# Chunked complex attention with a routed expert layer: expert weights loaded before the last units, factors gathered as rows, gates kept in place

## The chip, the cores and the metric

One core of one Trainium2 chip. The metric is device time of one execution in microseconds; the kernel before takes 468.15 us (median of 3 runs, 465.80 to 468.39).

## The reference

Two layers follow each other. The first is a recurrence with complex gates over 768 steps, for 4 batches x 8 heads of 48 channels; the second routes each of the 3072 tokens to at most one of 8 experts.

```python
mag = sqrt(a_re**2 + a_im**2);  scale = minimum(mag, 0.999) / (mag + 1e-6)
for t in range(768):              # S is complex, 48 x 48 for each batch and head
    S = (a_re + 1j*a_im)[t] * scale[t] * S + outer(k[t], v[t])
    y[t] = q[t] @ S.real
x = y as (3072, 384)
do = x @ w_skip > 0;  e = argmax(x @ w_gate);  g = softmax(x @ w_gate)[e]
out = x;  out[do] = x + g * (relu(x @ w1[e]) @ w2[e])   # w1: 384 x 1024, w2: 1024 x 384
```

## The kernel before, in words

**Units.** The sequence is cut into 6 chunks of 128 steps; a unit u = 4*c + b is one chunk c of one batch b, all 8 heads. Within a chunk the recurrence becomes matmuls: `pre(u)` (L158) loads the gates and turns them into log sizes U and a ratio r (Ln, Exp, a Square on ScalarE at L172, Ln, Exp; VectorE in between, with the test of L174 that marks gates too large for this path); `angle(u)` (L181) takes the arctangent of the ratio, sums it over the chunk with a matmul (L188) and makes sines and cosines cs; `size(u)` (L209) sums U with a matmul (L214) and makes e = exp(+-sum). `ready(u)` (L221) loads q and k, multiplies them by e (L232) and cs (L234) and transposes the results (tp, L239; copied by ScalarE at L240). `unit(u)` (L248) does the products: pa (L261) masked into at (L262), the state T carried over the chunks (RX L268, st L270, ps L274, T L277), py (L285, L288), and px (L293), which gives the output rows xa and the router's logits.

**Factors.** `factors(c)` (L199) needs the last row (step 127) of e and cs of the four units of a chunk, turned so that channels lie on partitions. L197 and L219 write those rows to DRAM, and six DMAs per chunk (L203, L205) read them back into G one 4-byte element at a time; L207 multiplies them into Fall, which the next chunk's RX reads.

**Order.** ScalarE's tables are switched twice per batch of four units: one phase for Ln and Exp (pre, size), one for Arctan and Sin (angle). Every piece gets a due time in units (`add(time, function)`, L475 on, with the gates AHEAD = 3 units before their own unit) and a scheduler turns due times and readiness into one instruction order per engine. SP issues all plain DMAs in one in-order queue; POOL issues the indirect ones.

**Routing and experts.** `route(c)` (L325) routes four units in one series of small VectorE operations; for the chunks that `last(c)` names (before: 4 and 5) `route1` (L389) does it unit by unit. Each ends in indirect DMAs on POOL (L322) that scatter the rows xa into the list xs, one after the other. px, ps and pr (the ranks within an expert) share one PSUM buffer (`ps_g`, tag g). In the first `route1` of chunk 5, `early` (L319) loads expert 0's first rows back from xs. `end` frees the gates' pools (ld, fe), in whose place m0 and mr come: `weights(0)` (L539) then loads expert 0's weights in seven pieces through two raw buffers (L551); ScalarE rounds each (L555), VectorE takes the remainder (L556). `tokens` (L568) collects expert 0's tokens by one-hot products (L591), and `moe` (L597) runs the experts: L620 and L643 to L645.

Of the kernel before, what the change touches and what calls it, by code (L numbers as in the profile page):

```python
# [9 lines left out]
F32 = mybir.dt.float32  # L10
# [15 lines left out]
BATCH = 4  # L26
AHEAD, TRIG, READY = 3.0, 1.0, 0.7
# [13 lines left out]
class Kern:  # L41
# [12 lines left out]
    def consts(self, ctx):  # L54
# [49 lines left out]
        self.G = cst.tile([96, NCH, 3, BH], F32, name="G")  # L104
# [53 lines left out]
    def pre(self, u):  # L158

        nc = self.nc  # L160
        V, A = nc.vector, nc.scalar
# [13 lines left out]
        V.scalar_tensor_tensor(la, la, 2.0, tr[:, 0], ALU.mult, ALU.add)  # L175
        self.table(tr[:, 0], la, AF.Exp, scale=-0.5, bias=self.lnw)
        U = self.U[u] = self.fe.tile([128, H, D], F32, name=f"U_{u}", tag="U", bufs=2 * BATCH)
        V.scalar_tensor_tensor(U, la, 0.0, tr[:, 0], ALU.min, ALU.subtract)
        self.tr[u] = tr

    def angle(self, u):  # L181
# [11 lines left out]
        cs = self.cs[u] = self.fe.tile([128, H, 2, D], F32, name=f"cs_{u}", tag="cs", bufs=BATCH + 2)  # L193
# [3 lines left out]
        nc.sync.dma_start(self.turns_at[c, b:b + 1], cs[127:128].rearrange("o h k d -> o (h k d)"))  # L197

    def factors(self, c):  # L199

        for r in range(2):
            g = self.G[r * D:(r + 1) * D, c]
            self.nc.sync.dma_start(g[:, 0], self.sizes_at[c].rearrange("b (h d) -> d (b h)", d=D))  # L203
            for k in range(2):
                self.nc.sync.dma_start(g[:, 1 + k], self.turns_at[c].rearrange("b (h k d) -> k d (b h)", d=D, k=2)[k])  # L205
        e = self.G[:, c, 0].unsqueeze(1).to_broadcast([96, 2, BH])
        self.nc.vector.tensor_tensor(self.Fall[:, c].rearrange("p k b h -> p k (b h)"), self.G[:, c, 1:3], e, ALU.mult)  # L207

    def size(self, u):  # L209

        nc = self.nc
        U = self.U.pop(u)
        pl = self.ps_c.tile([128, H, D], F32, name=f"pl_{u}", tag="c")
        nc.tensor.matmul(pl, self.mask, U, start=True, stop=True)  # L214
        e = self.e[u] = self.fe.tile([128, 2, H, D], F32, name=f"e_{u}", tag="e", bufs=BATCH)
# [3 lines left out]
        nc.sync.dma_start(self.sizes_at[c, b:b + 1], e[127:128, 0].rearrange("o h d -> o (h d)"))  # L219

    def ready(self, u):  # L221
# [4 lines left out]
        qk = self.ld.tile([128, 2, H, D], F32, name=f"qk_{u}", tag="qk", bufs=3)  # L226
# [17 lines left out]
    def last(self, c):  # L244

        return c // 2 == NG - 1

    def unit(self, u):  # L248
# [16 lines left out]
        if c > 0:  # L265
# [4 lines left out]
            V.scalar_tensor_tensor(Sb[:, :, 0:D], X[:, 1], self.sg, X[:, 0], ALU.mult, ALU.add)  # L270
# [184 lines left out]
    def attention(self):  # L455
        with ExitStack() as ctx:
# [4 lines left out]
            self.un, self.st = P("un", 2), P("st", 2)  # L461
# [7 lines left out]
            self.pr_ins, self.T, self.U, self.tr, self.cs, self.e, self.w = [{} for _ in range(7)]  # L469
# [27 lines left out]
            for k, us in enumerate(batches + [[]]):  # L497
# [16 lines left out]
            for k in range(1, 9):  # L514
                add(k // 3 + 0.2 + 0.25 * (k % 3), self.late, k)
            flat = [b[0] - AHEAD + 0.4 for b in batches]
            for u in range(n):
                if u not in batches[-1]:
                    add(u - READY, self.ready, u)
                else:  # L520
                    for k in range(2):
                        add(u + 0.5 + 0.25 * k, lambda: next(self.ws, None))
# [133 lines left out]
    def check(self, p, ps):  # L656
# [5 lines left out]
        with self.tc.issue_after(self.pins[1]):  # L662
# [10 lines left out]
            V.tensor_scalar(ok[:, 0, 0:B * NCH], self.over, 0.0, None, ALU.is_equal)  # L673
# [191 lines left out]
```

## Time and profile before

| | |
|---|---|
| median of 3 runs | 468.15 us |
| profiled execution, its own time | 470.65 us |
| its span, first to last instruction | 468.9 us |
| busy: PE / weight loads / VectorE / ScalarE / POOL | 396.7 / 351.4 / 330.3 / 299.7 / 66.4 us |
| DMA | 207010 packets, 68.77 MB; 184779 packets under 512 B |
| mean granted TensorE clock | 0.945 of full speed |

PE is TensorE's matmuls, PEld its weight loads (they overlap the matmuls), DVE VectorE, ACT ScalarE, SP the queue that issues DMAs. A matmul's shown length includes its way through the array, so that rows overlap; what one costs in a dense stretch is the distance from start to start. A bracket at a row's end is the idle time of its engine ahead of it, and what ended it. Line numbers L... are those of the kernel before; in the changed one the same code stands up to 5 lines lower or higher.

### The profile page before, as it was taken

The numbers are of one execution on the slowest core, as the hardware profiler recorded it, in microseconds if no ns is written. First come the engines' busy times: TensorE is split into PE (matmuls) and PEld (weight loads), VectorE is DVE, ScalarE is ACT, GpSimd is POOL, SyncE is SP. The second block draws the span as 40 slices with busy tenths as digits, with TensorE's granted clock in tenths as the row PEclk, the third lists the DMA queues.
The fourth block names the chain that finished last, engine by engine and source line by source line (L and its number), as shares of the span: only waits on it lengthen the run. The fifth ranks groups of instructions, "written<-read, shape, count | busy, mean of one in ns | idle before, by whom it ended". The sixth has DMA issues, their size and how long they took to land. (4 is left out here: it accounts for less than half of the span.)

```text
span 468.9 us, 8930 instructions
## 1 busy us (share of the span) xinstructions
PE 396.7 (85%) x3179; PEld 351.4 (75%) x3179; DVE 330.3 (70%) x780; ACT 299.7 (64%) x591; POOL 66.4 (14%) x94
## 2 busy tenths in 40 slices
PE   0698946999898989988997974498869999999994
PEld 0387832898787779767966863498869999999993
DVE  3467567987997898879979883447883667667331
ACT  6889859798978887896897262126652446446220
POOL 6000000000412012001201222200411010111011
PEclk9969967999999999999999996599989999999998
DMA  9999894992899489758507462356882685685000
GB/s 141 223 274 186 118 169 45 140 188 71 123 169 176 50 126 190 153 49 152 119 20 66 131 204 80 104 202 182 281 264 86 214 286 161 209 287 152 21 25 29
DMA packets 207010, 68.77 MB, mean 147 GB/s; under 512 B 184779, under 2 KB 202855, under 8 KB 206960
## 3 DMA queue, kind: packets, MB, share of 16 engines
q1 hardware_dynamic: 204400, 63.51, 62.9%
q0 software_dynamic: 2560, 4.63, 2.8%
q8 instruction: 27, 0.44, 0.4%
q14 instruction: 23, 0.19, 0.1%
HBM read 52.55 MB, written 15.88 MB: 146 GB/s over the span
## 5 line engine op out<-in xcount | busy, mean ns | idle before, releaser
L555 ACT CAST h<-r 128x768 fp32r<-128x768 f32 (+1 forms) x56 | 49.7, 925 | 37.1 <-DMA r<-in_moe_w_dram 20.9
L556 DVE TENSOR_TENSOR l<-r,h 128x768 fp32r<-128x768 f32 (+1 forms) x56 | 58.2, 1070 | 21.2 <-ACT h L555 21.0
L322 POOL DMA_INDIRECT xs<-xa,sl x24 | 32.0, 1333 | 232.1 <-ACT e L156 85.9
L239 PE MATMUL tp<-ident,w 128*96 128x128 f32 x384 | 56.7, 286 | 9.4 <-ACT wT L240 4.0
L240 ACT COPY wT<-tp 96x512 f32<-96x512 f32 x96 | 53.6, 591 | 14.6 <-PE tp L239 10.2
L239 PEld LDWEIGHTS tp<-ident,w 128*96 128x96 f32 x384 | 43.7, 132 | 19.5 <-ACT wT L240 8.5
L620 PE MATMUL ph<-xh,h 128*128 128x256 f32 x192 | 54.0, 287 | 4.3 <-DVE hl L623 3.7
L622 ACT ACTIVATE hh<-ph 128x256 fp32r<-128x256 f32 x64 | 23.5, 382 | 50.9 <-PE ph L620 48.0
L261 PE MATMUL pa<-wT,wT 96*128 96x128 f32 x384 | 53.4, 286 | 1.6 <-ACT wT L240 1.6
L620 PE MATMUL ph<-xh,l 128*128 128x256 f32 x192 | 53.8, 285 | 0.0
L261 PEld LDWEIGHTS pa<-wT,wT 96*128 96x128 f32 x384 | 47.9, 197 | 6.2 <-ACT wT L240 2.8
L620 PE MATMUL ph<-xl,h 128*128 128x256 f32 x192 | 51.5, 284 | 0.0
L285 PE MATMUL py<-at,vt 128*64 128x128 f32 x384 | 39.3, 292 | 9.1 <-DVE at L262 6.2
L234 DVE TENSOR_TENSOR w<-qk,cs 128x768 f32<-128x768 f32 x48 | 44.9, 947 | 0.0
L643 PE MATMUL po<-h,hh 128*128 128x384 f32 x128 | 44.0, 344 | 0.0
L644 PE MATMUL po<-l,hh 128*128 128x384 f32 x128 | 43.4, 339 | 0.0
L623 DVE SCALAR_TENSOR_TENSOR hl<-ph,hh 128x256 fp32r<-128x256 f32 x64 | 25.5, 418 | 25.4 <-ACT hh L622 24.4
L620 PEld LDWEIGHTS ph<-xh,h 128*128 128x128 f32 x192 | 36.6, 191 | 5.3 <-DVE hl L623 4.5
L293 PE MATMUL px<-wg,yT 128*128 128x105 f32 x192 | 28.2, 293 | 13.8 <-DVE m L420 10.8
L645 PE MATMUL po<-h,hl 128*128 128x384 f32 x128 | 39.7, 338 | 0.0
L293 PEld LDWEIGHTS px<-wg,yT 128*128 128x128 f32 x192 | 25.7, 206 | 16.0 <-DVE m L420 11.1
L620 PEld LDWEIGHTS ph<-xh,l 128*128 128x128 f32 x192 | 36.8, 191 | 0.0
(157 smaller groups left out, 831.3 us busy)
## 6 DMA issues: line engine op xcount, KB each, us to landing
r<-in_moe_w_dram SPq DMA_DIRECT2D x24, 512.0 KB
r<-in_moe_w_dram SPq DMA_DIRECT2D x32, 384.0 KB
ain<-in_a_re_dram SPq DMA_DIRECT2D x24, 192.0 KB
ain<-in_a_im_dram SPq DMA_DIRECT2D x24, 192.0 KB
qk<-in_q_dram SPq DMA_DIRECT2D x24, 192.0 KB
qk<-in_k_dram SPq DMA_DIRECT2D x24, 192.0 KB
vt<-in_v_dram SPq DMA_DIRECT2D x24, 192.0 KB
out_dram<-xa SPq DMA_DIRECT2D x24, 192.0 KB
```

The source lines that it names most:

```text
L234: V.tensor_tensor(n, qk[:, k].unsqueeze(2).to_broadcast([128, H, 2, D]), cs, ALU.mult)
L239: nc.tensor.transpose(tp[:, h], n[:, hh * 4 + h].rearrange("p k d -> p (k d)"), self.ident)
L240: A.copy(t[:, hh * 4:hh * 4 + 4], tp)
L261: PE.matmul(pa[:, h], kT[:, hh * 4 + h], qT[:, hh * 4 + h], start=True, stop=True)
L285: PE.matmul(py[j * 64:j * 64 + 64, hp], vt_[:, 2 * hp + j], at[:, 2 * hp + j], start=True, stop=(c == 0))
L293: pe = PE.matmul(px[:, hp], yT[:, hp], self.wg[:, hp], start=True, stop=True)
L555: nc.scalar.copy(hi[:, ks], raw)
L556: nc.vector.tensor_tensor(lo[:, ks], raw, hi[:, ks], ALU.subtract)
L620: pe = PE.matmul(ph, w[:, k, js], x[:, k], start=(n == 0), stop=(n == len(terms) - 1))
L643: PE.matmul(po, hh[:, j, sl], w2h[:, j], start=(j == 0), stop=False)
L644: PE.matmul(po, hh[:, j, sl], w2l[:, j], start=False, stop=False)
L645: pe = PE.matmul(po, hl[:, j, sl], w2h[:, j], start=False, stop=(j == NF - 1))
```

## The change

The gates' intermediate results go in place (into ain and tr) instead of la and sq; the square and the test become one VectorE instruction with a running maximum, and `check` compares that maximum at the end. q and k are multiplied by e in one instruction. The last rows go straight into an SBUF tile G of 4 partitions (each twice), and 24 transposes of 4 x 96 per chunk turn them; two ScalarE copies, one with the sign sg, and one VectorE product make Fall, so that st is a plain sum. AHEAD is 4. qk, cs and e move to a pool ff that outlives the gates; `end` and `weights(0)` come due from 16.5 units on, and only chunk 5 is routed unit by unit.

```diff
-AHEAD, TRIG, READY = 3.0, 1.0, 0.7
+AHEAD, TRIG, READY = 4.0, 1.0, 0.7
...                                     # pre: ain 6 buffers (4)
-        self.table(la, ain[:, 0], AF.Ln)
-        self.table(sq[:, 1], la, AF.Exp, scale=-1.0)
-        V.tensor_tensor(tr[:, 1], ain[:, 1], sq[:, 1], ALU.mult)
-        A.activation(sq[:, 0], tr[:, 1], AF.Square)
-        self.table(tr[:, 0], sq[:, 0], AF.Ln, scale=WIDE, bias=self.wide)
-        V.tensor_scalar(sq[:, 1], sq[:, 0], 2.4, None, ALU.is_gt, ALU.add, accum_out=self.over[:, u:u + 1])
+        re, im, s, r = ain[:, 0], ain[:, 1], tr[:, 0], tr[:, 1]
+        self.table(re, re, AF.Ln)
+        self.table(s, re, AF.Exp, scale=-1.0)
+        V.tensor_tensor(r, im, s, ALU.mult)
+        V.tensor_tensor_reduce(im, r, r, 1.0, 0.0, ALU.mult, ALU.max, accum_out=self.over[:, u:u + 1])
+        self.table(s, im, AF.Ln, scale=WIDE, bias=self.wide)
...
+    def gather(self, c, b, k, row):     # called by angle (k=0, cs) and size (k=1, e)
+        if c not in self.G:
+            self.G[c] = self.st.tile([B, 3 * H, 2, D], F32, name=f"G_{c}", tag="G", bufs=1)
+        rows = slice(0, 2 * H) if k == 0 else slice(2 * H, 3 * H)
+        for r in range(2):
+            self.nc.sync.dma_start(self.G[c][b:b + 1, rows, r], row)
     def factors(self, c):
...
+        pf = self.ps_g.tile([96, 3 * H, B], F32, name=f"pf_{c}", tag="g")
+        for h in range(3 * H):
+            nc.tensor.transpose(pf[:, h], G[:, h].rearrange("b r d -> b (r d)"), self.ident[0:B, 0:B])
+        e = self.st.tile([96, H, 2, B], F32, name=f"es_{c}", tag="es")
+        nc.scalar.copy(e[:, :, 0], pf[:, 2 * H:])
+        nc.scalar.activation(e[:, :, 1], pf[:, 2 * H:], AF.Copy, scale=self.sg)
+        nc.vector.tensor_tensor(..., ALU.mult)                  # Fall
...                                     # ready
+        V.tensor_tensor(qk, qk, e, ALU.mult)
         for k in range(2):
-            V.tensor_tensor(qk[:, k], qk[:, k], e[:, k], ALU.mult)
...
     def last(self, c):
-        return c // 2 == NG - 1
+        return c == NCH - 1
...                                     # unit
-            V.scalar_tensor_tensor(Sb[:, :, 0:D], X[:, 1], self.sg, X[:, 0], ALU.mult, ALU.add)
+            V.tensor_tensor(Sb[:, :, 0:D], X[:, 0], X[:, 1], ALU.add)
...                                     # attention: due times
-                        add(p - AHEAD + 0.22, self.factors, a // B - 1)
+                        add(a - 1.5, self.factors, a // B - 1)
...
-            add(batches[-1][0] - READY, end)
+            t = batches[-1][0] - AHEAD + 0.5
+            add(t, end)
+            for k in range(8):
+                add(t + 0.4 + 0.75 * k, lambda: next(self.ws, None))
```

**ScalarE ahead of unit 4**, from the last table load to the first copy of that unit's transposes (e_585 and its kin are units 4 to 7; la_618 and la_671 the Ln of units 8 and 9, sq their Exp). Before:

```order
L150 ACT_TABLE_LOAD
L156 ACTIVATE e_585<-pl_583,col 128x384 x2
L156 ACTIVATE la_618<-ain_615 128x384
L156 ACTIVATE e_591<-pl_589,col 128x384 x2
L156 ACTIVATE la_671<-ain_668 128x384
L156 ACTIVATE sq_619<-la_618 128x384
L156 ACTIVATE e_597<-pl_595,col 128x384 x2
L156 ACTIVATE sq_672<-la_671 128x384
L156 ACTIVATE e_603<-pl_601,col 128x384 x2
L240 COPY wT_4_836<-tp_4_0_837 96x512
```

and now (two Ln, of units 8 and 9, and the first e stand ahead of these rows):

```order
L153 ACTIVATE ain_652<-ain_652 128x384
L153 ACTIVATE ain_748<-ain_748 128x384
L153 ACTIVATE e_491<-pl_489,col 128x384 x2
L295 COPY yT_3_829<-py_3_820 128x512
L210 COPY es_786<-pf_761 96x8x4
L211 ACTIVATE es_786<-pf_761,sg 96x8x4
L153 ACTIVATE tr_513<-ain_510 128x384
L153 ACTIVATE tr_560<-ain_557 128x384
L153 ACTIVATE e_498<-pl_496,col 128x384 x2
L153 ACTIVATE tr_655<-ain_652 128x384
L153 ACTIVATE tr_751<-ain_748 128x384
L245 COPY wT_4_880<-tp_4_0_881 96x512
```

Eight steps of the next batch stand ahead of unit 4 instead of four, with the two copies of the factors; the sizes of unit 7 and the output copies of unit 3 have moved behind.

**SP's queue at the end of the attention.** Before (r_0 are the pieces of expert 0's weights, xa_3330 the output rows of chunk 5, `early` the load back from xs):

```order
L551 DMA r_0_0_3338<-in_moe_w_dram 128x1024
L551 DMA r_0_1_3361<-in_moe_w_dram 128x1024
L281 DMA T_3_3082<-T_3_3082 48x384 x2
L256 DMA vt_151<-in_v_dram 128x8x48
L551 DMA r_0_2_3410<-in_moe_w_dram 128x1024
L308 DMA out_dram<-xa_2622 128x384
L551 DMA r_0_0_3432<-in_moe_w_dram 128x2x384
L551 DMA r_0_2_3481<-in_moe_w_dram 128x2x384
L308 DMA out_dram<-xa_3330 128x384
L551 DMA r_0_4_3501<-in_moe_w_dram 128x2x384
L319 DMA early<-xs 128x2x384
L551 DMA r_0_6_3550<-in_moe_w_dram 128x2x384
```

and now, from the piece before the last one on (qk_3463 is unit 23's):

```order
L552 DMA r_0_4_3296<-in_moe_w_dram 128x2x384
L261 DMA vt_150<-in_v_dram 128x8x48
L286 DMA T_2_2962<-T_2_2962 48x384 x2
L232 DMA qk_3463<-in_q_dram 128x8x48
L233 DMA qk_3463<-in_k_dram 128x8x48
L313 DMA out_dram<-xa_2706 128x384
L552 DMA r_0_6_3398<-in_moe_w_dram 128x2x384
```

The last piece stood behind `early`; now all seven stand ahead of the values of units 22 and 23, and `early` follows 14 rows later, behind the first two output rows of chunk 5.

**PE at the end of the attention**, from unit 22's px to the one-hot products (pr are the ranks, pf the transposes of the factors, here those of chunk 5, which only `check` reads). Before:

```order
L293 MATMUL px_2_3472<-wg,yT_2_3470 128x105 x4
L407 LDWEIGHTS tri
L407 MATMUL pr_2_3492<-oh_2_3486,tri 128x8
L408 LDWEIGHTS ones
L408 MATMUL pr_2_3492<-ohs,ones 128x8
L591 MATMUL pt_0_3653<-ohx,xa_3330 128x128 x3
```

and now:

```order
L298 MATMUL px_2_3454<-wg,yT_2_3452 128x105 x4
L208 MATMUL pf_3497<-ident,G_2580 96x4 x24
L412 LDWEIGHTS tri
L412 MATMUL pr_2_3533<-oh_2_3527,tri 128x8
L413 LDWEIGHTS ones
L413 MATMUL pr_2_3533<-ohs,ones 128x8
L592 MATMUL pt_0_3687<-ohx,xa_3256 128x128 x3
```

The 24 transposes stand between px and pr, all three in the one buffer of `ps_g`.

## Rows read from the trace of the kernel before

**Rows 1.** Four stretches of the whole span (windows); columns: stretch, its length, then busy time and number of instructions of PE, of the weight loads PEld, of DVE, ACT and POOL, then the granted clock of TensorE as a share of full speed, the mean busy share of the 16 DMA engines and GB/s.

```profile
20.00:94.00 74.00, 59.48 (x418) 47.47 (x420) 55.71 (x114) 61.20 (x126) 0.19 (x1) 0.84 0.91 162
94.00:262.00 168.00, 155.24 (x1467) 129.94 (x1464) 145.93 (x366) 138.52 (x288) 23.94 (x17) 1.00 0.68 117
262.00:312.00 50.00, 32.84 (x292) 30.19 (x291) 29.31 (x131) 16.42 (x31) 11.45 (x11) 0.80 0.48 149
312.00:469.00 157.00, 143.40 (x1003) 141.53 (x1002) 92.65 (x158) 70.00 (x127) 23.25 (x24) 0.98 0.52 168
```

**Rows 2.** Waits by pair in the stretch 50 to 100 us (engine and line, what it waited for, us in total, times, longest).

```profile
ACT tr L156 <- DVE la L175: 6.3, 2, 5.8
DVE Fall L207 <- DMA G<-turns_at: 5.6, 1, 5.6
```

**Rows 3.** ACT in order of time, 50 to 100 us (start, us, engine, line, operation, out<-in, count, and in brackets the idle time before it and what ended it). The first row is the last Exp of pre for unit 6, the second the first copy of unit 4's transposes.

```profile
62.49 0.61 ACT L156 ACTIVATE tr<-la,col 128x384 f32<-128x384 f32 x1 [5.80 <-DVE la L175]
...
83.05 0.60 ACT L240 COPY wT<-tp 96x512 f32<-96x512 f32 x1
```

**Rows 4.** PE in order of time, 50 to 100 us.

```profile
56.76 1.56 PE L274 MATMUL ps<-vt,w 128*96 128x48 f32 x16
63.11 1.12 PE L285 MATMUL py<-at,vt 128*64 128x128 f32 x8 [4.79 <-DVE at L262]
...
81.57 1.78 PE L239 MATMUL tp<-ident,w 128*96 128x128 f32 x8
```

**Rows 5.** Groups of instructions by line and shape, the whole span (busy us, mean ns of one | idle before).

```profile
L234 DVE TENSOR_TENSOR w<-qk,cs 128x768 f32<-128x768 f32 x48 | 44.9, 947 | 0.0
...
L556 DVE TENSOR_TENSOR l<-r,h 128x768 fp32r<-128x768 f32 x32 | 29.5, 958 | 13.7 <-ACT h L555 13.5
...
L232 DVE TENSOR_TENSOR qk<-qk,e 128x384 f32<-128x384 f32 x48 | 25.4, 550 | 9.5 <-ACT e L156 6.3 <-DMA qk<-in_q_dram 2.4 <-DMA qk<-in_k_dram 0.8
...
L555 ACT CAST h<-r 128x768 fp32r<-128x768 f32 x32 | 25.2, 832 | 27.4 <-DMA r<-in_moe_w_dram 18.4 <-PE po L645 8.9
...
L175 DVE SCALAR_TENSOR_TENSOR la<-la,tr 128x384 f32<-128x384 f32 x24 | 13.1, 550 | 1.6 <-ACT tr L156 1.5
...
L174 DVE TENSOR_SCALAR_CACHE_REDUCE sq<-sq 128x384 f32<-128x384 f32 x24 | 12.9, 543 | 0.6 <-ACT sq L172 0.6
L172 ACT ACTIVATE sq<-tr 128x384 f32<-128x384 f32 x24 | 12.8, 543 | 2.7 <-DVE tr L171 2.7
...
L270 DVE SCALAR_TENSOR_TENSOR st<-RX,sg 96x384 f32<-96x384 f32 x20 | 12.2, 608 | 0.4 <-PE py L288 0.3
...
L277 DVE TENSOR_TENSOR T<-st,ps 96x384 f32<-96x384 f32 x16 | 8.7, 543 | 6.8 <-PE ps L274 6.8
...
L305 ACT COPY lg<-px 128x36 f32<-128x36 f32 x16 | 3.1, 193 | 1.2 <-PE px L293 1.2
...
L174 DVE DVE_READ_ACCUMULATOR sq<-sq 128x1 f32 x24 | 1.9, 79 | 0.0
...
L451 DVE SCALAR_TENSOR_TENSOR todo<-m 128x1 f32<-128x1 f32 x8 | 1.2, 153 | 0.0
```

**Rows 6.** PE in order of time, 94 to 140 us: the 16 matmuls of one unit's kv product, whose weights are 96 columns wide, and the row that starts behind them.

```profile
99.56 1.56 PE L274 MATMUL ps<-vt,w 128*96 128x48 f32 x16
100.95 2.02 PE L261 MATMUL pa<-wT,wT 96*128 96x128 f32 x16
```

**Rows 7.** Waits of 262 to 345 us.

```profile
ACT h L555 <- DMA r<-in_moe_w_dram: 20.9, 13, 9.5
...
DVE l L556 <- ACT h L555: 16.0, 7, 9.7
```

**Rows 8.** SP's queue of DMA issues in order of time, 255 to 345 us (start, time until the next, engine, line).

```profile
280.31 0.37 SPq L551 DMA_DIRECT2D r<-in_moe_w_dram  x1
291.42 0.37 SPq L319 DMA_DIRECT2D early<-xs  x1
291.89 0.40 SPq L551 DMA_DIRECT2D r<-in_moe_w_dram  x1
```

**Rows 9.** PE in order of time, 262 to 316 us: px of units 20, 22 and 23 (unit 21 lies between), the first one-hot product of expert 0 (L591) and the first matmul of expert 0 (L620).

```profile
275.90 1.14 PE L293 MATMUL px<-wg,yT 128*128 128x105 f32 x8 [0.26 <-DVE m L420]
...
298.30 2.04 PE L293 MATMUL px<-wg,yT 128*128 128x105 f32 x8 [8.66 <-DVE m L420]
...
301.69 2.91 PE L591 MATMUL pt<-ohx,xa 128*128 128x128 f32 x12
304.39 1.31 PE L293 MATMUL px<-wg,yT 128*128 128x105 f32 x8
...
311.78 0.39 PE L620 MATMUL ph<-xh,h 128*128 128x256 f32 x1 [0.57 <-ACT xh L593]
```

**Rows 10.** POOL in order of time, 225 to 345 us: the scatters of routed rows into xs, each a DMA; the last of the four rows waits for the load early (L319) to have read xs.

```profile
279.80 1.02 POOL L322 DMA_INDIRECT xs<-xa,sl  x1 [2.17 <-ACT yT L290]
285.04 1.55 POOL L322 DMA_INDIRECT xs<-xa,sl  x1 [4.21 <-ACT h L555]
288.75 0.97 POOL L322 DMA_INDIRECT xs<-xa,sl  x1 [2.16 <-DMA xs<-xa,sl]
295.23 0.97 POOL L322 DMA_INDIRECT xs<-xa,sl  x1 [5.51 <-DMA early<-xs]
```

**Rows 11.** One stretch in the windows view, with the granted clock (the columns of Rows 1).

```profile
285.00:305.00 20.00, 9.32 (x61) 8.59 (x61) 6.79 (x42) 3.08 (x7) 5.44 (x5) 0.50 0.24 80
```

More of the change, by code (lines that the diff above doesn't have):

```diff
@@ L103, in consts @@
         self.Fall = cst.tile([96, NCH, 2, B, H], F32, name="Fall")
-        self.G = cst.tile([96, NCH, 3, BH], F32, name="G")
         self.ohs = cst.tile([128, E], BF16, name="ohs")
@@ L192, in angle @@
         V.scalar_tensor_tensor(tr[:, 0], y, -1.0, y, ALU.mult, ALU.max)
-        cs = self.cs[u] = self.fe.tile([128, H, 2, D], F32, name=f"cs_{u}", tag="cs", bufs=BATCH + 2)
+        cs = self.cs[u] = self.ff.tile([128, H, 2, D], F32, name=f"cs_{u}", tag="cs", bufs=2 * BATCH)
         self.table(cs[:, :, 1], y, AF.Sin, scale=-2 * math.pi)
@@ L196, in angle @@
         c, b = divmod(u, B)
-        nc.sync.dma_start(self.turns_at[c, b:b + 1], cs[127:128].rearrange("o h k d -> o (h k d)"))
-    def factors(self, c):
[L201 to L207, printed above, removed]
+        self.gather(c, b, 0, cs[127:128].rearrange("o h k d -> o (h k) d"))
+    def gather(self, c, b, k, row):
[4 more added lines that the diff above has]
+            self.nc.sync.dma_start(self.G[c][b:b + 1, rows, r], row)
+    def factors(self, c):
+        nc = self.nc
+        G = self.G.pop(c)
+        pf = self.ps_g.tile([96, 3 * H, B], F32, name=f"pf_{c}", tag="g")
[4 more added lines that the diff above has]
+        nc.scalar.activation(e[:, :, 1], pf[:, 2 * H:], AF.Copy, scale=self.sg)
+        nc.vector.tensor_tensor(self.Fall[:, c].rearrange("p k b h -> p h k b"), pf[:, 0:2 * H].rearrange("p (h k) b -> p h k b", k=2), e, ALU.mult)
     def size(self, u):
@@ L214, in size @@
         nc.tensor.matmul(pl, self.mask, U, start=True, stop=True)
-        e = self.e[u] = self.fe.tile([128, 2, H, D], F32, name=f"e_{u}", tag="e", bufs=BATCH)
+        e = self.e[u] = self.ff.tile([128, 2, H, D], F32, name=f"e_{u}", tag="e", bufs=BATCH + 1)
         for k in range(2):
@@ L218, in size @@
         c, b = divmod(u, B)
-        nc.sync.dma_start(self.sizes_at[c, b:b + 1], e[127:128, 0].rearrange("o h d -> o (h d)"))
+        self.gather(c, b, 1, e[127:128, 0])
     def ready(self, u):
@@ L225, in ready @@
         c, b = divmod(u, B)
-        qk = self.ld.tile([128, 2, H, D], F32, name=f"qk_{u}", tag="qk", bufs=3)
+        qk = self.ff.tile([128, 2, H, D], F32, name=f"qk_{u}", tag="qk", bufs=3)
         nc.sync.dma_start(qk[:, 0], self.rows(self.q, c, b))
@@ L468, in attention @@
                 nc.gpsimd.memset(t[:, :, D:64], 0.0)
-            self.pr_ins, self.T, self.U, self.tr, self.cs, self.e, self.w = [{} for _ in range(7)]
+            self.pr_ins, self.T, self.U, self.tr, self.cs, self.e, self.w, self.G = [{} for _ in range(8)]
             n = B * NCH
@@ L487, in end @@
             def end():
-                for u in batches[-1]:
-                    self.at(u - READY)
-                    self.ready(u)
                 self.rctx.close()
@@ L514, in attention @@
             for k in range(1, 9):
-                add(k // 3 + 0.2 + 0.25 * (k % 3), self.late, k)
+                add(0.8 + 0.3 * k, self.late, k)
             flat = [b[0] - AHEAD + 0.4 for b in batches]
             for u in range(n):
[L518 to L522, printed above, removed]
+                add(u - READY, self.ready, u)
                 add(u, unit, u)
@@ L526, in attention @@
                 elif u % B == B - 1:
-                    add(next(p for p in flat if p > u + 0.5), route, u)
-            add(batches[-1][0] - READY, end)
+                    add(next((p for p in flat if p > u + 0.5), u + 0.7), route, u)
+            t = batches[-1][0] - AHEAD + 0.5
+            add(t, end)
+            for k in range(8):
+                add(t + 0.4 + 0.75 * k, lambda: next(self.ws, None))
             for t, f, a in sorted(todo, key=lambda x: x[0]):
@@ L672, in check @@
             V.tensor_reduce(fl[:, 0:1], ok, AX.XY, ALU.min)
-            V.tensor_scalar(ok[:, 0, 0:B * NCH], self.over, 0.0, None, ALU.is_equal)
+            V.tensor_scalar(ok[:, 0, 0:B * NCH], self.over, 2.4, None, ALU.is_le)
             V.tensor_reduce(fl[:, 1:2], ok, AX.XY, ALU.min)
```

16 lines of the change are left out of this document (6 added, 10 removed).

## The prediction

> **What bounds the kernel now.** I read the windows first [rows 1]. They show three kinds of stretch. From 94 to 262 us, units 4 to 19, PE is busy 155.24 of 168 us while VectorE has 145.93 and ScalarE 138.52: PE sets the pace there, and the gaps come to 12.8 us. Before that, from 20 to 94 us, PE has 59.48 of 74 us and ScalarE 61.20; after it, from 262 to 312 us, PE has 32.84 of 50 us and nobody else has more: that is waiting. From 312 us on the experts run on PE at 143.40 of 157 us, and the change has nothing there. So I then read the two loose stretches for what ends their waits.
>
> In the first, the waits by pair name one DMA: VectorE stands 5.6 us at the product Fall until the element-wise loads of the factors land [rows 2], and behind it in VectorE's in-order queue stands la, for which ScalarE idles 5.80 us [rows 3]. ScalarE must still do the Exp, the angle phase and the sizes of units 4 to 7 before unit 4 can be transposed: PE's first transposes of unit 4 start at 81.57 us, though the previous unit's kv product ran at 56.76 us [rows 4].
>
> In the last, ScalarE's rounding of expert 0's weights waits up to 9.5 us for a DMA, and VectorE's remainder behind it 9.7 us [rows 7]. SP's queue tells why: one piece is issued at 280.31 us, the last at 291.89 us, right behind `early` at 291.42 us [rows 8], which waits for the scatters [rows 10]. VectorE holds unit 22's routing behind that remainder, and PE waits 8.66 us for px of unit 22 [rows 9]. In the 20 us from 285 us on TensorE runs at the lower of its two levels, 1.2 GHz (0.50) [rows 11].
>
> **The change part by part.** The sum is made against the profiled execution, 470.65 us with a span of 468.9 us; the median of the runs shown is 2.5 us lower.
>
> *A, up to unit 4's transposes.* The element loads go, and with them the 5.80 us of ScalarE's idle time [rows 3]: -5.8. Their successors are 96 row copies; the first chunk's are issued on SP well ahead of the transposes, so Fall waits for its own two copies on ScalarE instead. Each of the 8 units so far loses its square on ScalarE, 0.543 us as a row, some 0.45 from start to start [rows 5]: -3.6. By the order four more steps of the next batch stand ahead of unit 4, at the same price: +1.8, and two copies of the factors, like the logits copy of 0.193 [rows 5]: +0.4. The sizes of unit 7 (two steps) and two copies of unit 3 go behind, priced like the square and the logits copy: -1.6. Sum -8.8. The gates' loads, which are late next, now stand ahead of q's in SP's queue.
>
> *B, from there to the last chunk.* PE gets 24 transposes per chunk, four times: each loads weights 96 columns wide. The nearest rows are 16 such loads in 100.95 - 99.56 = 1.39 us, 0.087 each [rows 6]: 24 x 0.087 = 2.1 us, four times +8.4. Bounds: the row behind it, with loads 128 wide, has 2.02 us for 16, 0.126 each, which makes 3.0; half the price of the nearest row, since only 4 columns stream through, makes 1.0. The kv product and px of unit 3 now come behind unit 4's transposes: +2.5 (1.39 [rows 6] and 1.14 [rows 9]). Against that stand the 12.8 us of gaps. ScalarE loses 16 squares (-7.2) and gains the copies (+1.6) and the seven roundings moved in here, 0.83 us each and a third more for three of them [rows 5] (+6.6): about level. VectorE: merging the two products by e saves 2 x 0.550 - 0.947 = 0.15 us per unit, -2.4; st as a plain sum costs 0.543 as T's row does, not 0.608, -1.0; chunk 4 routed as one series instead of four, each of 18 operations at 0.153 us, saves 3 x 18 x 0.153 = -8.3; the seven remainders, 0.958 us and more [rows 5], add +7.5. So VectorE has about 4 us less. What can fill PE's gaps is the look-ahead of one more unit and the deeper buffers; I take two thirds of 12.8 us, -8.5. Sum +2.4.
>
> The fused square and maximum has no row. Its bounds are the accumulating instruction that it replaces on VectorE, 0.543 + 0.079 us for the read of the accumulator, and the same with the time of a product of 768 elements, 0.947 + 0.079 [rows 5]. I take the lower one: L175, which reads two fp32 tiles of this size from SBUF, takes 0.550, and L174, which accumulates, 0.543; only the two together are new. At that price VectorE gives nothing away.
>
> The Trainium skill speaks against this part: "Vector Engine (DVE) Microarchitecture Reference", section "Points that are easy to get wrong", says that an instruction of the scalar-tensor-tensor kind with two sources in SBUF that are not bf16 runs at half throughput, since both read ports are taken and none is left for the accumulator. The trace agrees only in part: without an accumulator such an instruction keeps the full rate (L175), with both no run here shows it. By that rule the upper bound holds.
>
> *C, from px of unit 20 to expert 0.* Before, this takes 311.78 - 275.90 = 35.9 us [rows 9]. All seven pieces of the weights are now issued ahead of `early`, so the wait for the last one goes: -8.7 [rows 9]. With PE fed, the lower level of the clock goes: 9.32 us busy at half speed [rows 11] would be half as long; I take -4 of 4.7, since short waits stay. Four remainders of 0.96 us leave VectorE's queue, half of them on the path: -2. Added on the path: the transposes of the last chunk's factors between px and pr of unit 22, in the same PSUM buffer, 2.1 us, with two copies and a product that must read them before pr may write, 0.6: +2.7. And `early` now waits for the four scatters of chunk 4, all issued after its one routing series, about when px of unit 20 runs. Scatters stand (288.75 - 279.80) / 2 = 4.5 us apart, from the last to `early` are 2.7 us, to the end of its read 3.8 [rows 8, 10]: 3 x 4.5 + 6.5 = 20 us. The product that needs it is reached 28.5 - 8.7 - 4 - 2 = 13.8 us (px of unit 20 to px of unit 23, less the gains), plus 2.7, plus 2.6 for px and one group of one-hot products: 19.1. Nearly equal; I add +1.5. Sum -10.5.
>
> *D, the experts.* The second expert's weights follow the last output rows in SP's queue as before: 0.
>
> Total: -8.8 + 2.4 - 10.5 = -16.9, so 453.8 us for an execution like the profiled one, and 451 us as a median.
>
> **The rivals.**
> 1. *PE keeps its gaps.* The transposes and the moved work come on top of a stretch that is PE's already, and the look-ahead fills nothing: B is +10.9, total -8.4, 460 us as a median. For it: every pf waits for readers on two engines. Against it: PE's gaps are ends of short chains, which an earlier batch removes.
> 2. *The look-ahead gives more.* PE's rows overlap, so 155 us busy hold real slack; if ScalarE and VectorE stop holding it, the gaps close (-12.8 in B) and as much as another 8 us go: B is -9.9, total -29.2, 439 us.
> 3. *The fused instruction runs at half rate.* 24 x 0.40 = 9.7 us more on VectorE, two thirds of it on the path: 458 us. By the Trainium skill's rule above the time would come out so.
> 4. *Slower: the single PSUM buffer.* pf sits in `ps_g` until ScalarE and VectorE have read it, and PE, in order, stands at the next px, ps or pr. Price: 2.1 us of transposes, about 2 us of ScalarE's queue (four steps) and 2.8 of VectorE's (three rows of 0.947 ahead), 6.9 us in each of 6 chunks, 41 us less the 11 counted already, so 30 above the forecast: 481 us. It decides from about 5 us a chunk on. For it: Fall stands behind three long VectorE rows in the new order. Against it: these waits are hidden where other PE work stands between.
> 5. *No change.* That the weights are not really earlier is excluded by the order; left is a scatter chain that grows with the traffic beside it and eats C, with rival 1: 467 us.
>
> **How the numbers follow.** Forecast 47%, rival 1 15%, rival 2 14%, rival 3 11%, rival 4 9%, rival 5 4%. Half a per cent, 2.3 us, is what a measurement of this kernel can tell. Faster by more: forecast and rivals 1 to 3, 0.87; same: 0.04; slower: 0.09. The range goes from 437, just under rival 2, to 465, over rivals 1 and 3 and the upper bound of the transposes; outside lie rivals 4 and 5 and the far side of rival 2.
>
> **What would show it.** Right: no wait of Fall on a DMA; unit 4's transposes near 73 us; no wait of the roundings over 2 us before expert 0; px of unit 20 to expert 0 in about 25 us, at the full clock; pf's 24 transposes in 1 to 3 us; the fused instruction near 0.55 us. Wrong: PE waiting several microseconds in each chunk for Fall or es; VectorE above PE in the middle stretch; the product with `early` waiting long for its load.

## The result and the profile after

The changed kernel takes 452.64 us (median of 4 runs, 451.51 to 454.06) beside 466.98 us (465.68 to 468.39) for the kernel before: a ratio of 0.9694, 95% interval 0.9648 to 0.9740. The ratios of the experiments below leave out the profiled execution and any over 1.5% above the fastest of its kernel; medians and ranges have them all. The profiled execution took 454.06 us, span 452.3 us, so the sum of the prediction, 453.8 us, stands beside 454.06. Its terms do not all stand like that. They are cut here at unit 4's first transposes, px of unit 20 and expert 0's first matmul:

| stretch | before | forecast | after | difference |
|---|---|---|---|---|
| A, to unit 4's transposes | 81.57 | -8.8 | 72.22 | -9.35 |
| B, to px of unit 20 | 194.33 | +2.4 | 202.01 | +7.7 |
| C, to expert 0 | 35.88 | -10.5 | 25.56 | -10.3 |
| D, to the end of the span | 157.12 | 0 | 152.51 | -4.6 |

B and C in the windows view, with the columns of [rows 1], before (the first two rows) and after:

```profile
81.57:275.90 194.33, 177.37 (x1678) 149.75 (x1676) 170.56 (x427) 154.23 (x317) 26.98 (x19) 1.00 0.70 123
275.90:311.78 35.88, 22.11 (x180) 20.41 (x181) 16.89 (x94) 10.21 (x20) 8.40 (x8) 0.71 0.41 132
72.22:274.23 202.01, 189.21 (x1791) 163.94 (x1792) 175.59 (x383) 153.85 (x323) 28.53 (x19) 0.95 0.63 126
274.23:299.79 25.56, 22.07 (x210) 20.79 (x209) 13.41 (x90) 6.55 (x18) 5.83 (x6) 0.87 0.37 124
```

Four stretches of the span after, in the same view; the borders follow the work, not the clock time of before.

```profile
20.00:94.00 74.00, 62.82 (x468) 51.74 (x468) 53.00 (x99) 66.31 (x136) 0.27 (x1) 0.84 0.84 170
94.00:245.00 151.00, 141.38 (x1320) 121.60 (x1322) 132.40 (x297) 120.12 (x251) 22.87 (x16) 0.94 0.66 128
245.00:295.00 50.00, 46.06 (x488) 42.73 (x485) 37.77 (x131) 20.28 (x47) 10.52 (x8) 0.93 0.40 107
295.00:452.30 157.30, 145.85 (x1042) 144.22 (x1040) 94.74 (x167) 71.12 (x129) 25.84 (x27) 0.99 0.54 179
```

The loose stretch ahead of the experts is filled: PE is busy 46.06 of its 50 us, where it had 32.84 of 50. New is the clock of the middle, 0.94 instead of 1.00.

PE after, in order of time: the factors' transposes of chunk 0 and unit 4's first transposes (for [rows 4]), the two stalls of the middle, and then px of unit 20, the first rank product of unit 22, the product with `early` and expert 0 (for [rows 9]).

```profile
68.64 1.28 PE L208 MATMUL pf<-ident,G 4*96 4x4 f32 x24
72.22 1.94 PE L244 MATMUL tp<-ident,w 128*96 128x128 f32 x8 [1.07 <-DVE w L239]
...
97.64 0.69 PE L290 MATMUL py<-at,vt 128*64 128x128 f32 x4 [4.03 <-issue]
...
195.40 2.80 PE L279 MATMUL ps<-vt,w 128*96 128x48 f32 x16 [3.75 <-DVE cand L373]
...
274.23 1.04 PE L298 MATMUL px<-wg,yT 128*128 128x105 f32 x8
...
288.60 0.17 PE L412 MATMUL pr<-oh,tri 128*128 128x8 bf16 x1 [0.76 <-DVE Fall L212]
...
294.90 1.50 PE L592 MATMUL pt<-ident,early 128*128 128x128 f32 x12
...
299.79 0.39 PE L621 MATMUL ph<-xh,h 128*128 128x256 f32 x1 [0.57 <-ACT xh L594]
```

The rounding of expert 0's weights, which waited up to 9.5 us [rows 7], waits 0.6 us at most from 245 to 300 us (one of 2.4 us, over the 2 us that the prediction named, ends earlier, at 242.67 us):

```profile
ACT h L556 <- DMA r<-in_moe_w_dram: 0.9, 2, 0.6
```

The 20 us from 285 us, at 0.50 of the clock before [rows 11], have 0.83. In the same view, the stretch in which SP issues chunk 1's row copies, and the two stretches around the stalls:

```profile
76.20:87.60 11.40, 10.34 (x103) 9.48 (x101) 11.40 (x25) 9.35 (x20) 0.00 (x0) 1.00 0.14 32
92.00:104.00 12.00, 7.82 (x56) 6.43 (x56) 8.96 (x18) 5.36 (x12) 0.00 (x0) 0.72 1.17 181
190.00:204.00 14.00, 10.25 (x67) 9.62 (x66) 11.51 (x34) 10.46 (x22) 0.06 (x1) 0.76 0.72 127
285.00:305.00 20.00, 17.56 (x140) 17.20 (x139) 7.89 (x46) 4.19 (x12) 3.88 (x4) 0.83 0.47 159
```

SP's queue from 76 to 93 us says what the prediction did not count. The 16 row copies go out as two blocks, 11.3 us together, with no load between; the 16 DMA engines have a busy share of 0.14 meanwhile. The loads of q and k stand behind them (those of unit 7 are shown), and VectorE waits 5.71 us for k:

```profile
76.20 5.78 SPq L200 DMA_DIRECT2D G<-cs  x8
82.07 5.53 SPq L200 DMA_DIRECT2D G<-e  x8
...
90.09 0.66 SPq L232 DMA_DIRECT2D qk<-in_q_dram  x1
90.80 0.69 SPq L233 DMA_DIRECT2D qk<-in_k_dram  x1
```

```profile
95.04 0.96 DVE L236 TENSOR_TENSOR qk<-qk,e 128x768 f32<-128x768 f32 x1 [5.71 <-DMA qk<-in_k_dram]
...
96.85 0.68 DVE L267 TENSOR_TENSOR at<-pa,mask 128x512 f32<-128x512 f32 x1
...
193.73 0.96 DVE L236 TENSOR_TENSOR qk<-qk,e 128x768 f32<-128x768 f32 x1 [2.49 <-DMA qk<-in_k_dram]
...
195.16 0.19 DVE L373 TENSOR_TENSOR cand<-oh,pr 128x32 f32<-128x32 bf16 x1
```

`at` and `cand` stand behind these waits in VectorE's queue, and PE's two stalls end right behind them: py needs `at`, and ps needs the PSUM buffer that `cand` reads. G has one buffer, so a chunk's 16 copies must follow the transposes of the chunk before; whether a second one would spread them was not run.

The new instructions, by line and shape (the columns of [rows 5]):

```profile
L236 DVE TENSOR_TENSOR qk<-qk,e 128x768 f32<-128x768 f32 x24 | 22.9, 952 | 17.4 <-DMA qk<-in_k_dram 11.2 <-ACT e L153 6.2
...
L168 DVE CUSTOM_DVE_ANT_0 ain<-tr 128x384 f32<-128x384 f32 x24 | 13.0, 552 | 0.1
...
L208 PE MATMUL pf<-ident,G 4*96 4x4 f32 x144 | 7.9, 185 | 1.1 <-ACT xa L311 1.1
...
L168 DVE DVE_READ_ACCUMULATOR2_ANT over<- 128x1 f32 x24 | 2.0, 81 | 0.0
```

### The profile page after: what moved, and what is told of

Its sections match the earlier page's. It is cut to its first block, busy times and chain, and to the rows that moved or that the text cites. A ratio compares the mean times of both kernels' runs of the same rounds, so it can differ in the third digit from the quotient of the medians.

```text
span 452.3 us, 9133 instructions
## 1 busy us (share of the span) xinstructions
PE 401.4 (89%) x3320; PEld 362.5 (80%) x3320; DVE 324.8 (72%) x706; ACT 290.5 (64%) x580; POOL 67.3 (15%) x94
## 5 line engine op out<-in xcount | busy, mean ns | idle before, releaser
L244 PE MATMUL tp<-ident,w 128*96 128x128 f32 x384 | 60.5, 293 | 9.5 <-DVE w L239 5.6
L327 POOL DMA_INDIRECT xs<-xa,sl x24 | 34.9, 1454 | 219.4 <-DVE w L239 72.8
L244 PEld LDWEIGHTS tp<-ident,w 128*96 128x96 f32 x384 | 46.1, 137 | 15.8 <-DVE w L239 6.8
L266 PE MATMUL pa<-wT,wT 96*128 96x128 f32 x384 | 57.1, 296 | 0.5 <-ACT wT L245 0.5
L266 PEld LDWEIGHTS pa<-wT,wT 96*128 96x128 f32 x384 | 51.6, 207 | 4.2 <-issue 2.0
L279 PEld LDWEIGHTS ps<-vt,w 128*96 128x96 f32 x320 | 32.5, 177 | 8.9 <-DVE cand L373 3.8
L279 PE MATMUL ps<-vt,w 128*96 128x48 f32 x320 | 32.8, 258 | 5.5 <-DVE cand L373 3.7
```

The source lines that it names most:

```text
L244: nc.tensor.transpose(tp[:, h], n[:, hh * 4 + h].rearrange("p k d -> p (k d)"), self.ident)
L266: PE.matmul(pa[:, h], kT[:, hh * 4 + h], qT[:, hh * 4 + h], start=True, stop=True)
L279: PE.matmul(ps[:, h], kw[:, h].rearrange("p k d -> p (k d)"), vt_[:, h, 0:D], start=True, stop=True)
```

## The experiments

Each ran 4 times beside the kernel before, whose median was 466.8 to 467.4 us; the ratio is to that. A is the time at which unit 4's transposes start and B to D are lengths, as in the table above, from each profiled execution. Those of e1 and e8 are the slowest of their four (457.40 and 450.01 us), so they are read for places, not for sizes.

| run | median (range), us | ratio, interval | A | B | C | D |
|---|---|---|---|---|---|---|
| e1 copies on POOL | 451.68 (448.92-457.40) | 0.9642, 0.9587-0.9697 | 73.8 | 199.6 | 25.7 | 156.5 |
| e2 copies doubled | 488.54 (485.93-489.45) | 1.0443, 1.0382-1.0504 | 75.8 | 225.6 | 30.1 | 154.8 |
| e3 weights late | 452.71 (451.59-453.63) | 0.9680, 0.9632-0.9729 | 73.3 | 199.8 | 25.6 | 152.6 |
| e4 element factors | 446.49 (445.58-447.57) | 0.9545, 0.9498-0.9592 | 81.1 | 185.8 | 25.7 | 153.3 |
| e5 buffers late | 460.24 (458.92-461.02) | 0.9870, 0.9800-0.9941 | 72.9 | 194.3 | 37.2 | 154.9 |
| e6 four routes | 461.07 (460.03-462.14) | 0.9891, 0.9820-0.9963 | 73.6 | 210.1 | 25.6 | 151.0 |
| e7 square on ScalarE | 456.24 (454.97-456.91) | 0.9785, 0.9717-0.9853 | 72.0 | 203.6 | 27.4 | 152.1 |
| e8 rows for chunk 0 | 446.94 (442.83-450.01) | 0.9565, 0.9473-0.9657 | 72.9 | 196.5 | 23.4 | 155.4 |
| e9 transposes doubled | 473.52 (471.72-476.04) | 1.0156, 1.0091-1.0221 | 72.9 | 215.2 | 27.5 | 154.3 |
| e10 copies on ScalarE | 510.92 (510.36-513.75) | 1.0959, 1.0888-1.1030 | 91.4 | 238.8 | 26.5 | 152.0 |
| e11 look-ahead 3 | 454.08 (449.45-457.11) | 0.9667, 0.9579-0.9755 | 71.2 | 202.8 | 25.7 | 153.3 |
| e12 before, early weights | 456.05 (454.81-459.38) | 0.9755, 0.9696-0.9814 | 82.7 | 198.9 | 19.7 | 156.4 |

### The row copies: e1, e2, e10, e9, e4, e8

**e1**, copies on GpSimd's queue:

```diff
-            self.nc.sync.dma_start(self.G[c][b:b + 1, rows, r], row)
+            self.nc.gpsimd.dma_start(self.G[c][b:b + 1, rows, r], row)
```

> All row copies of the factors are issued on GpSimd's queue instead of SP's; nothing else is changed. Theory Q (SP's queue is the price of the row copies: in each chunk it issues 16 of them in some 11 us, issues nothing else meanwhile, the DMA engines stand idle, and the loads of q and k behind them come late, so that PE stood 4.03 us at 93.6 us and 3.75 us at 191.6 us, each time followed by the lower clock): both stalls go, the stretch from unit 4's transposes to px of unit 20 falls from 202 us to 194 to 198, total 445 to 449 us. Rival W (the stretch is longer for PE's own work: transposes and moved products; late loads are a symptom): 451 to 454. Rival P (GpSimd, which writes the descriptors itself and holds the scatters behind them, makes the factors or the scatters late): 455 or more, with Fall or the load early waiting.

451.68 us: no difference that can be told. An issue costs GpSimd 0.5 us, and the copies stand among its scatters. The 16 of a chunk still take 8 us. The first of the rows is POOL in order of time:

```profile
123.69 0.64 POOL L304 COPY xa<-tok 128x4 f32<-128x4 f32 x1 [2.02 <-DMA xs<-xa,sl]
124.39 3.96 POOL L200 DMA_DIRECT2D G<-cs  x8
128.32 3.08 POOL L200 DMA_DIRECT2D G<-e  x6
```

Between 60 and 300 us k still came late (7.7 us), and PE now stood for the sizes:

```profile
DVE qk L236 <- DMA qk<-in_k_dram: 7.7, 5, 3.1
...
PE pl L219 <- ACT e L153: 4.7, 4, 1.9
```

Theory Q in its plain form, that SP's hold alone is the price, fell here.

**e2**, each copy twice on SP:

```diff
-        for r in range(2):
+        for r in (0, 1, 0, 1):
```

> Every row copy of the factors is issued twice on SP (32 instead of 16 a chunk). Theory Q: SP is held 22 us of each chunk's 45, q and k come late in nearly every chunk, the stretch from unit 4 to px of unit 20 grows by 10 to 30 us, total 462 to 482 us. Rival W: only SP is busier, nothing waits for it longer: 452 to 455.

488.54 us, 36 more, above Q's range. SP stays with the copies 20 us at a stretch:

```profile
86.64 9.36 SPq L200 DMA_DIRECT2D G<-cs  x15
...
97.43 9.74 SPq L200 DMA_DIRECT2D G<-e  x14
```

More issues on SP do cost time, and rival W (SP is only busier) fell. By which way is not settled: of the 23.6 us that B grew, 16.4 are PE's busy time (205.64 us at 0.87 of the clock), VectorE waits less for k than in the changed kernel (8.5 us from 72 to 288 us, there 11.2), and ScalarE waits 4.5 us until the copies have read e.

**e10**, copies on ScalarE's queue (`nc.scalar.dma_start` in the same line):

> All row copies are issued on ScalarE's queue, right behind the instructions that write the rows; all else as in the changed kernel. SP is free and GpSimd's scatters stand behind no copy. Theory Q with issues that cost ScalarE little: 444 to 448 us. Theory Q with issues that hold ScalarE as they hold SP, 0.7 us each, 11 us a chunk on an engine that has some 10 of 45 free: 455 to 470.

510.92 us, worse than the range. An issue costs ScalarE 0.6 us as it costs SP, 10.5 us in one block, and nothing of ScalarE's own runs in it:

```profile
142.61 5.12 ACTq L200 DMA_DIRECT2D G<-cs  x8
147.76 5.42 ACTq L200 DMA_DIRECT2D G<-e  x8
153.23 1.12 ACT L153 ACTIVATE ain<-ain,col 128x384 f32<-128x384 f32 x2 [10.70 <-DMA G<-e]
```

Behind them the factors' copies es are late, Fall with them, and PE stands at the next ps, which wants the same PSUM buffer:

```profile
207.93 2.76 PE L279 MATMUL ps<-vt,w 128*96 128x48 f32 x16 [8.13 <-DVE Fall L212]
```

That is the mechanism of the prediction's rival 4, in a kernel in which ScalarE is late; in the changed kernel PE waits 0.76 us for Fall, once.

**e9**, each transpose of the factors twice:

```diff
-        for h in range(3 * H):
+        for h in list(range(3 * H)) * 2:
```

> Each of the 24 transposes of the factors runs twice, in all six chunks (1.28 us more of PE a time in the changed kernel's rows); all else as there. Theory W (the transposes are PE time on the path in the stretch that PE fills): 6 times 1.28 less what fits into gaps, +5 to +8, total 458 to 461 us. Theory Q (SP's hold is the price, and the transposes fall into the gaps that it makes): +0 to +3, total 452 to 456.

473.52 us: 21 more, far over both. The 48 take 2.4 us instead of 1.28, so 7 us of the 21 are PE's own. Between 72 and 288 us VectorE waits 16.3 us for k (11.2 in the changed kernel), and ScalarE 6.2 us in one wait until the copies have read a row of e; the granted clock of B is 0.93 (0.95 there), and the order of PE's work differs too. What makes up the rest is not settled.

**e4**, factors through DRAM by element loads, as before; the other edits of the change stay:

```diff
-        self.gather(c, b, 1, e[127:128, 0])
+        nc.sync.dma_start(self.sizes_at[c, b:b + 1], e[127:128, 0].rearrange("o h d -> o (h d)"))
...
-            nc.tensor.transpose(pf[:, h], ...)      # and es, Fall from pf
+            self.nc.sync.dma_start(g[:, 1 + k], self.turns_at[c].rearrange("b (h k d) -> k d (b h)", d=D, k=2)[k])
...                                                  # likewise the sizes; st with sg again; factors due as before
```

> The factors go through DRAM and come by element-wise loads, as in the kernel before, without the 24 transposes per chunk; all else as in the changed kernel. Theory A: Fall waits on those loads again ahead of unit 4, 5 to 6 us; against it SP has 14 issues a chunk instead of 16 and PE 1.3 us a chunk less: total 450 to 457 us. Rival (the row copies carry most of the gain): 460 or more, with Fall waiting for a DMA in every chunk.

446.49 us, 6.2 less than the changed kernel and under its own range: **the row copies with their transposes cost time.** The wait that they were to remove is back, longer than before:

```profile
DVE Fall L213 <- DMA Gs<-turns_at: 8.7, 1, 8.7
```

Unit 4 starts 8.9 us later, and B is 16.2 us shorter: PE is idle 5.73 us of it instead of 12.80, at 0.98 of the clock instead of 0.95:

```profile
81.10:266.92 185.82, 180.09 (x1698) 154.29 (x1697) 170.53 (x378) 151.64 (x312) 37.83 (x19) 0.98 0.73 129
```

Added up over B, the changed kernel's 80 row copies hold SP 51.0 us; the 62 issues in their place hold it 30.3 us and stand among the loads, and from 72 to 268 us VectorE never waits for k.

**e8**, row copies for chunk 0 alone, element loads from chunk 1 on:

```diff
+        if c > 0:
+            at = self.sizes_at if k else self.turns_at
+            self.nc.sync.dma_start(at[c, b:b + 1], row.rearrange("o r d -> o (r d)"))
+            return
...                                                  # factors(c): the element loads for c > 0
```

> Row copies and transposes make the factors of chunk 0 alone, where Fall otherwise waits for its loads with nothing beside it; the other chunks' factors go through DRAM and come by element-wise loads, as in the kernel before (one small VectorE product more per chunk for the sign). All else as in the changed kernel. Theory Q2 (row copies gain some 9 us ahead of unit 4 and lose 16 behind it, by 16 issues on SP and 24 transposes on PE in every chunk): both gains together, unit 4's transposes near 73 us and from there to px of unit 20 186 to 190 us, total 437 to 442 us. Rival (the 9 us ahead of unit 4 come back in the next stretch, since only the work's place moves): 445 to 448.

446.94 us (442.83 to 450.01): within its spread the same as e4, the rival's case. Unit 4 starts 8.2 us earlier than in e4, and px of unit 20 no earlier (269.5 us, e4 266.9). Counted from 20 us, PE is idle 20.0 of 246.9 us up to there in e4 (46.84 + 180.09 busy) and 21.7 of 249.5 in e8 (44.48 + 183.27): the idle time moved from the Fall wait to later places. The two differ in one thing more: e8's Gs has one buffer for all chunks, e4's one for each.

```profile
72.92:269.46 196.54, 183.27 (x1700) 156.66 (x1700) 175.39 (x388) 153.64 (x316) 34.17 (x19) 0.97 0.72 128
```

### The weights: e3, e5, e12

**e3**, `end` and the weights' steps due late, as before:

```diff
-            t = batches[-1][0] - AHEAD + 0.5
-            add(t, end)
-            for k in range(8):
-                add(t + 0.4 + 0.75 * k, lambda: next(self.ws, None))
+            for u in batches[-1]:
+                for k in range(2):
+                    add(u + 0.5 + 0.25 * k, lambda: next(self.ws, None))
+            add(batches[-1][0] - READY, end)
```

> The buffers of the gates are given up, and expert 0's weights loaded, as late as in the kernel before; all else as in the changed kernel. Theory C (10 us of the gain come from px of unit 20 to expert 0, because the last load of the weights no longer stands behind the load early): this stretch goes from 25.6 back to about 36 us, less the four routing series that are one now, so 33 to 36; total 460 to 463 us. Rival (the stretch shrank since the routing of chunk 4 is one series and the factors need no loads): 25 to 28 us there, total 452 to 455.

452.71 us, and the loads still ran at 236 to 254 us: the edit did not do what it says, for the scheduler issues a load as soon as its buffers are free. It says that the due times are not the cause, and nothing on the weights. PE's order is that of the changed kernel, instruction by instruction, so the two also show how far one execution's stretches scatter: A by 1.1 us, B by 2.2.

**e5**, the buffers late as well:

```diff
-        cs = self.cs[u] = self.ff.tile(...)          # e likewise; qk from self.ld
+        cs = self.cs[u] = self.fe.tile(...)
...                                                  # and the edit of e3, ready(u) of the last batch ahead of the pools' end
```

> The run e3 left the weights' loads at 236 to 254 us, since the buffers of q and k, of the angles' rows and of the sizes were no longer among those given up; here these three go back to the gates' pools, and the pools are given up only behind the last batch's products, so that expert 0's weights are loaded in the last chunk again, the last piece behind the load early. All else as in the changed kernel. Theory C: px of unit 20 to expert 0 takes 33 to 36 us instead of 25.6, total 460 to 463 us. Rival (chunk 4 as one routing series, which empties VectorE's queue, made the stretch short): 25 to 28 us, total 451 to 455.

460.24 us. C is back at 37.2 us (forecast 33 to 36), with the same signature as before: the last piece behind `early`, and the lower clock. All the weights' work of ScalarE and VectorE is back in C with it.

```profile
286.78 0.37 SPq L324 DMA_DIRECT2D early<-xs  x1
287.26 0.40 SPq L556 DMA_DIRECT2D r<-in_moe_w_dram  x1
```

```profile
285.00:305.00 20.00, 13.31 (x102) 13.08 (x102) 7.55 (x44) 3.81 (x10) 3.89 (x4) 0.66 0.45 152
```

But B is 7.8 us shorter than in the changed kernel: early weights bring 11.7 us in C and cost 7.8 in B. Theory C stands for its stretch; the net is 3.9 us from unit 4 to expert 0 in these two executions and 7.6 by the medians, most of the rest in D.

**e12**, the kernel before with this edit alone (pool ff, early `end`):

> The kernel before, with one edit of the change: the buffers of q and k, of the angles' rows and of the sizes lie in a pool of their own, the gates' pools are given up ahead of the last batch, and expert 0's weights are loaded and split there. By e5 (these weights bring 12 us behind px of unit 20, cost 7 ahead of it and 2 less in the experts): 457 to 461 us. Rival (VectorE, which still routes chunk 4 in four series here, has no room for the remainders): 464 to 470.

456.05 us, 11 less than before and a little under its range: the largest single part, and it needs none of the others. C is 19.7 us here.

### Routing, square, look-ahead: e6, e7, e11

**e6**, chunk 4 by four series:

```diff
-        return c == NCH - 1
+        return c // 2 == NG - 1
```

> Chunk 4 is routed by four single series again, as in the kernel before; all else as in the changed kernel. The three more series cost VectorE 8 us between units 16 and 20. Theory C: VectorE has that room (38 of 50 us busy in the stretch from 245 us), so 453 to 456 us. Rival: VectorE's queue decides in the last chunks, 459 to 463 us, or, since the scatters of chunk 4 start earlier and early with them, 449 to 451.

461.07 us: 8.4 more, and B is 8.1 us longer. VectorE is busy 5.3 us longer in B (180.88 after 175.59), less than the 8.3 us at which the prediction priced the three series; PE is idle 4.0 us longer and busy 4.1 longer, at 0.93 of the clock. The first theory, that VectorE has that room, was wrong. PE's stop at 245 us and the clock around it:

```profile
245.41 2.73 PE L279 MATMUL ps<-vt,w 128*96 128x48 f32 x16 [2.92 <-DVE m L425]
```

```profile
240.00:260.00 20.00, 13.80 (x97) 12.74 (x96) 14.86 (x51) 7.46 (x12) 3.42 (x3) 0.66 0.56 152
```

PE waits for the PSUM buffer that L425, a step of one unit's routing, has to read first, and L425 stands in VectorE's queue behind products and remainders.

**e7**, the square on ScalarE and the test on VectorE again:

```diff
-        V.tensor_tensor_reduce(im, r, r, 1.0, 0.0, ALU.mult, ALU.max, accum_out=self.over[:, u:u + 1])
+        A.activation(im, r, AF.Square)
+        V.tensor_scalar(s, im, 2.4, None, ALU.is_gt, ALU.add, accum_out=self.over[:, u:u + 1])
```

> The fused square and maximum becomes two instructions again, the square on ScalarE and an accumulating test on VectorE; all else as in the changed kernel. ScalarE gets 24 squares of 0.543 us, VectorE's work stays. By the term for the squares (0.45 us each for 8 units up to unit 4's transposes, hidden beyond) the total is 454 to 457 us. Rival (the fused one is no gain): 452 to 453. Rival (ScalarE's chain decides in every chunk): 460 or more.

456.24 us, 3.6 more, as the term said in size; not in place, for A is unchanged (72.0) and the time appears in B and C.

**e11**, AHEAD = 3:

> The planner's look-ahead goes back from 4 units to 3; all else as in the changed kernel. By the term for PE's gaps (the look-ahead and the deeper buffers fill two thirds of 12.8 us): 456 to 461 us. Rival (the gaps of the changed kernel come from late loads, which a longer look-ahead doesn't mend): 450 to 454.

454.08 us (449.45 to 457.11): within its spread no different, and PE is idle 12.1 us of B (12.8 in the changed kernel). The look-ahead gives nothing that can be told.

## Why the prediction was right, and where it was not

**The total** came out since two misses cancel, B's of +5.3 us and D's of -4.6: that is luck. It also rests on a profiled execution of before that lay 3.7 us over its median; by medians the gain is 14.3 us. Undone one at a time, by the medians, the parts are worth: early weights 7.6 us, chunk 4 in one series 8.4, the fused instruction 3.6, the look-ahead 1.4 (unclear), the row copies and transposes -6.2. The sum is 14.8; that they add up so well is partly luck, since the parts share the same idle time: early weights alone bring 11 us (e12). The merged product by e, the gates kept in place, the other buffer counts and due times were not undone alone.

**A** was forecast at -8.8 and is -9.35: no wait of Fall on a DMA, unit 4 at 72.22 us (forecast 73). The split failed. With the element loads back (e4) A grows by 8.9 us, so the row copies in their place are worth more in A than the 5.8 taken; with the squares back on ScalarE (e7) A does not move, so their -3.6 is not there. What failed besides is the step that counts A as gain. e8 beside e4 says that a start 8 us earlier at unit 4 is lost again by px of unit 20, as far as e8's spread lets it be told. The wait was the last to end in its own stretch, and PE's next stretch had room for the delay.

**B** was mis-sized, +2.4 against +7.7. Transposes: 1.28 us a chunk, less than the 2.1 taken and inside the bounds. Gaps: PE is idle 12.8 us of B (202.01 - 189.21), before 17.0 (194.33 - 177.37), so 4.2 were filled and not 8.5; "the look-ahead" as the filler fell with e11, "the deeper buffers" were not undone. PE's busy time grew by 11.8 us, while the transposes (four times 1.28) and the moved products (2.5) make 7.6. No term had the clock of B, 0.95 instead of 1.00. As an estimate from these figures, that is 20 us more at the lower of its two levels, half speed, so up to 10 us of PE's time, enough for the miss of 5.3. Missing too was SP's time: "well ahead of the transposes" was read from the order, and the 16 issues of 0.6 us each (0.7 from start to start) had no term. Two stalls of PE of about 4 us follow late loads, each with a granted clock of 0.72 to 0.76 around it. Yet e1, without that block on SP, is no faster, so how the 6.2 us divide between transposes, issues and clock stays open. The weights' work was called "about level"; e5 puts it at 7.8, in one execution. And chunk 4's one series was one line of a VectorE sum there; of what was undone, e6 shows it to be the largest gain of the stretch.

**C** was right in size, 25.56 us, forecast about 25, and the late weights were the cause: e5 brings them and the 11.7 us back, and e6, where C is 25.6, excludes the routing of chunk 4. That the wait behind `early` is most of it is argued; e5 moves all the weights' work. The split differs: PE's busy time is the same (22.11 and 22.07 us), and all the gain is idle time, 13.8 us before and 3.5 after. So nothing is left of the clock's -4 in the sum beside the added work; the clock came back to 0.83 in the 20 us from 285, not to the full level. `early` was not late, and its +1.5 did not show: the scatters of chunk 4 stand 3.2 us apart (275.57 to 285.24 us), not 4.5, its read was over by 292.28 us, when POOL's next scatter starts, and PE reaches the product at 294.90.

```profile
292.28 0.97 POOL L327 DMA_INDIRECT xs<-xa,sl  x1 [6.07 <-DMA early<-xs]
```

**D** was forecast at 0 and came out at -4.6, which covered B's miss. The experts' code is the same. Before, PE waits once 2.11 us for `hl` 37 us into D, and the ten us from 348 us have 0.83 of the clock; after, no wait for `hl` is over 0.57 us.

```profile
349.01 0.39 PE L620 MATMUL ph<-xh,h 128*128 128x256 f32 x1 [2.11 <-DVE hl L623]
```

D scatters from 151.0 to 156.5 us over the profiled executions with the change, and the kernel before and e12, built on it, have 157.1 and 156.4 (e12 with the same wait of 2.11 us). With one profile of each, chance and an effect of the change can't be told apart.

**Rivals.** Rival 1 (PE keeps its gaps) is the nearer story for B, though 4.2 us of the gaps were filled and the clock is not in it. Rival 2 (the gaps close and more) is out: 12.8 us of them are left, and in e11 the look-ahead gives nothing. Rival 3 is out: the fused instruction takes 0.552 us and 0.081 for the accumulator, the forecast's lower bound. The Trainium skill's rule of half throughput ("Vector Engine (DVE) Microarchitecture Reference", "Points that are easy to get wrong") does not show; it appears here as a custom instruction with one tile as both sources, and the rule may be meant for another form. Rival 4 did not happen, and e10 shows its mechanism at work.

## What to carry to other kernels

Undo each part of a combined change: here the part with the best story (no more element loads) loses 6 us, and e4, without it, beats both kernels at 446.49 us. Give every DMA issue its time on the queue that issues it, and ask which loads stand behind the block. Price a wait that stands ahead of a stretch paced by another engine at what the end of that stretch moves: here 8 us at its start moved nothing that can be told at its end (e8 beside e4).

## What the runs showed of the hardware

A row copy of 3 or 1.5 KB from one partition holds the issuing queue 0.59 or 0.63 us on SP (medians of cs and e), 0.60 or 0.62 on ScalarE and 0.51 on GpSimd, while the DMA engines are nearly idle. The Trainium skill ("DMA: Bandwidth & Descriptors", "Issuing engines are not separate DMA queues") calls the sequencer's time to start a DMA usually small beside the DMA itself. For these it is not: from 76 to 88 us SP is full and the engines have a share of 0.14. The same row of cs written to DRAM, in one piece, holds SP 0.25 us (the kernel before, and e4); in G it lies in 16 pieces of 192 bytes. Whether the pieces or the target make the difference was not run.

The Trainium skill says ("Perfetto Trace Analysis", "DMA Optimizations") that balancing DMAs over the engines that can issue them may help where descriptor generation is the bottleneck. A split over queues was not run; moving all the copies gave nothing on GpSimd (e1) and cost 58 us on ScalarE (e10), whose own instructions wait behind the issues.
